# Attention and a gated two-layer network on one core: the places of the tiles in SBUF are taken in another order

## The chip, the core and the metric

The kernel runs on one core of a Trainium2 chip. The metric is the device time in microseconds (us) of one execution. Three executions of the kernel before were timed; their median is the figure to be compared with.

## The reference

Attention over a narrow band and over block summaries comes first, for 4 batches, 8 heads, 768 positions and 64 elements a head; its output, 3072 rows of 512, goes through two matrix products with a softmax and a normalisation between them.

```python
k_sum = k.reshape(B, H, nb, 32, D).max(axis=3)
v_sum = v.reshape(B, H, nb, 32, D).mean(axis=3)
scores_l = where(|i - j| < 16, q @ k.T / sqrt(D), -1e9)
scores_s = q @ k_sum.T / sqrt(D) + log(32)
a = softmax(concatenate([scores_l, scores_s]))
x = a @ concatenate([v, v_sum])          # [3072, 512] after the heads are joined
h = x @ w_in                             # 512 -> 1024
solu = h * softmax(h)
ln = (solu - mean) / sqrt(var + 1e-6) * g_ln
out = ln @ w_out                         # 1024 -> 512
```

All of it is float32.

## The kernel before, in words

The rows are worked in 24 tiles of 128 (`t` from 0 to 23). For each tile there are six pieces of work on TensorE: the scores `s` (line 578), their transposes `t` (line 633), the weighted sum of the values `x` (line 672), the first product `h` (line 697), the transposes `lt` of the normalised rows (line 633 again) and the second product `o` (line 775).

The two products are where float32 accuracy is bought with three passes. Each operand is split into a high and a low part in the type float32r, and three matmuls are added up in PSUM: high data with low weights, low data with high weights, high with high. A matmul has a part that is loaded into the array first, by LDWEIGHTS, and a part that is streamed through it. Here the **data** (`xh`, `xl` for `h`; `lh`, `ll` for `o`; 128 columns, 512 bytes in each partition) are loaded, and the **weights** (`w0` to `w15`; 512 columns, 2048 bytes) are streamed. One tile takes 24 matmuls for `h` and 24 for `o`, so 576 and 576 in all; the last tile's `o` is cut into two column halves, which makes 48 matmuls of 256 columns out of its 24.

`w0` to `w7` are `w_in`, `w8` to `w15` are `w_out`; each tile holds a high half of 2048 bytes and a low half of 2048 bytes, and stands in the place of the raw words it was split from. The data tiles exist twice and are used in turn: `xh` and `xl` change place with every second tile (a group of 256 positions feeds two tiles), `lh` and `ll` with every tile.

The order of all instructions comes from a planner (`Plan`): work is first recorded as operations with an estimated cost, then `issue` orders them, in 64 trials with noise, by these costs, and writes the best order out. While TensorE would have nothing to do early on, `keep_up` writes bfloat16 matmuls of a tile of zeros (`zero`, line 900) to keep it running.

A tile's place in SBUF is taken when its buffer is touched for the first time (`Buf.ap`, line 60, calls the `make` that `Plan.buf`, line 93, stored). So in the kernel before the places follow one another in the order in which the planner wrote the first use of each buffer out, and small tiles of 4 to 192 bytes lie between the large ones. Places are rounded to 32 bytes.

Of the kernel before, what the change touches and what calls it, by code (L numbers as in the profile page):

```python
# [13 lines left out]
BF16 = mybir.dt.bfloat16  # L14
# [6 lines left out]
P = 128  # L21
# [30 lines left out]
class Buf:  # L52


    def __init__(self, make, prev=()):
        self.make, self.prev, self.tile = make, prev, None
        self.ops, self.writers, self.readers, self.gone = [], {}, {}, False
# [15 lines left out]
class Plan:  # L73
# [14 lines left out]
    TRIES, NOISE = 64, 3.0  # L88

    def __init__(self):  # L90
        self.ops, self.rings, self.banks, self.idle = [], {}, {}, None

    def buf(self, pool, shape, dtype, tag, bufs, name):
        ring = self.rings.setdefault(tag, [])
        slot = f"{tag}_{len(ring) % bufs}"
        b = Buf(lambda: pool.tile(shape, dtype, tag=slot, bufs=1, name=name), ring[-bufs:][:1] if len(ring) >= bufs else ())
        ring.append(b)
        return b

    def place(self, make, bank, tag):  # L100

        b = Buf(make, [self.banks[bank]] if bank in self.banks else ())
        self.banks[bank] = b
        self.rings.setdefault(tag, []).append(b)
        return b
# [149 lines left out]
def attn_then_solu(ctx: ExitStack, tc: tile.TileContext, q, k, v, vr, vb, w_in, w_out, g_ln, out):  # L255
# [3 lines left out]
    nc = tc.nc  # L259
    plan = Plan()  # L260
# [13 lines left out]
    const = ctx.enter_context(tc.tile_pool(name="const", bufs=1))  # L274
# [21 lines left out]

    mask = const.tile([P, 3, KC], F32, name="mask")
    g_sb = const.tile([P, NFC], F32, name="g_sb")
    zero = const.tile([P, 512], BF16, name="zero")

    make_identity(nc, ident)
    nc.gpsimd.memset(mhalf, -0.5)
    nc.vector.memset(zero, 0.0)
    nc.gpsimd.memset(mask[:, :, :WIN], 0.0)
    nc.gpsimd.memset(mask[:, :, WIN:], math.log(BLOCK) / SCALE)
    for p0 in (0, QT):
# [531 lines left out]
    for t in range(NT):  # L838
        n, j = divmod(t, 2)
        b, g = its[n]  # L840
# [59 lines left out]
        nc.tensor.matmul(x[:, :n], zero[:, :P], zero[:, :n], start=True, stop=True)  # L900

    plan.idle = idle
    plan.issue()


# [38 lines left out]
```

## Time and profile before

| | |
|---|---|
| median of the three timed executions | 397.99 us (lowest 396.39, highest 946.64) |
| the profiled execution | 397.45 us, its span from first to last instruction 395.7 us |
| TensorE matmuls busy | 386.6 us, 98% of the span |
| weight loads busy | 298.3 us, 75% |
| VectorE, ScalarE, GpSimd busy | 275.4, 248.7, 97.9 us |
| mean granted TensorE clock | 0.999 of full |

PE is TensorE's matmuls, PEld its LDWEIGHTS, DVE is VectorE, ACT ScalarE, POOL GpSimd, SP the engine that issues most loads. A recorded matmul lasts longer than its share of TensorE's time, since matmuls are pipelined: a matmul of 512 columns is recorded with 380 to 400 ns, but the next one starts 216 to 237 ns after it. The time from one start to the next, called the spacing below, is what adds up to the kernel's time. It is read from a stretch of time that begins and ends at matmul starts, as the length of the stretch over the number of matmuls, or of weight loads, in it.

### The profile page before, as it was taken

The page shows a single profiled execution, that of the slowest core. Times are in us where ns is not written, and L with a number is a line of the kernel's source. Part 1 is how long each engine was busy: PE and PEld are TensorE (multiplying, and loading weights), DVE is VectorE, ACT ScalarE, POOL GpSimd, SP SyncE. Part 2 cuts the span into 40 slices and gives each one's busy share as a digit, 9 for nine tenths or more (in the row PEclk, how much of TensorE's full clock was granted, in tenths as well). Part 3 has the DMA queues.
Part 4 walks back from the last instruction along what each step waited for, and adds up shares of the span by engine and source line. Part 5 has one row for each costly group of instructions (what it writes and reads, how often), then busy time and mean ns, then how long its engine had stood idle before and what let it go on. Part 6 is the DMA issues. An engine that isn't in the chain of part 4 may idle for free.

```text
span 395.7 us, 9677 instructions
## 1 busy us (share of the span) xinstructions
PE 386.6 (98%) x3697; PEld 298.3 (75%) x3703; DVE 275.4 (70%) x884; ACT 248.7 (63%) x746; POOL 97.9 (25%) x245
## 2 busy tenths in 40 slices
PE   8999998999999999999999999999999999999996
PEld 3436766677878888878888888878888887878776
DVE  4999998999789866577767657657657654554330
ACT  3889686999798756658558466468466463533411
POOL 4224010416837221236220121221021021101100
PEclk9999999999999999999999999999999999999999
DMA  7999992136277320463330410430310000000011
GB/s 287 411 410 369 409 329 78 56 113 185 70 248 208 113 103 0 141 175 104 123 112 2 150 66 27 156 73 28 108 48 27 2 28 27 16 12 28 27 55 53
DMA packets 14994, 49.24 MB, mean 124 GB/s; under 512 B 1836, under 2 KB 2092, under 8 KB 13412
## 3 DMA queue, kind: packets, MB, share of 16 engines
q1 hardware_dynamic: 11084, 41.89, 30.8%
q10 hardware_dynamic: 3864, 6.74, 4.7%
q8 instruction: 29, 0.48, 0.5%
q14 instruction: 17, 0.14, 0.1%
HBM read 40.11 MB, written 6.29 MB: 117 GB/s over the span
## 4 chain that ended last, share of the span: by engine, by line
PE 85%; DMA 6%; ACT 3%; DVE 2%; issue 1%; ACTq 1%; SPq 1%; DVEq 0%
PE o L775 35%; PE h L697 30%; PE x L672 6%; PE s L578 5%; PE t L633 3%; PE lt L633 3%; DMA st_v<-in_vr 3%; DMA raw<-in_w_in 2%; DMA vt<-vsum 2%; PE vs_ps L459 1%; PE x L900 1%; ACT he L712 1%; DVE he L720 1%; ACT at L281 1%; PE x L664 1%
## 5 line engine op out<-in xcount | busy, mean ns | idle before, releaser
L775 PE MATMUL o<-w,lh 128*128 128x512 f32 (+1 forms) x400 | 128.0, 390 | 0.1
L697 PE MATMUL h<-w,xh 128*128 128x512 f32 x384 | 127.0, 398 | 0.4 <-DVE he L720 0.4
L605 ACT ACTIVATE e<-e,nm 128x120 f32<-128x120 f32 x192 | 73.1, 385 | 25.0 <-DVE nm L597 25.0
L775 PEld LDWEIGHTS o<-w,lh 128*128 128x128 f32 x400 | 74.1, 188 | 18.5 <-issue 2.4
L697 PEld LDWEIGHTS h<-w,xh 128*128 128x128 f32 x384 | 72.1, 188 | 18.9 <-ACT e L605 0.8
L775 PE MATMUL o<-w,ll 128*128 128x512 f32 (+1 forms) x200 | 76.9, 384 | 0.0
L697 PE MATMUL h<-w,xl 128*128 128x512 f32 x192 | 75.6, 394 | 0.0
L707 DVE TENSOR_REDUCE hm<-h 128x1 f32<-128x512 f32 x48 | 32.6, 686 | 42.7 <-PE h L697 42.7
L281 ACT COPY at<-t 120x512 f32<-120x512 f32 x46 | 24.8, 587 | 46.1 <-PE t L633 45.6
L775 PEld LDWEIGHTS o<-w,ll 128*128 128x128 f32 x200 | 37.6, 188 | 6.6
L697 PEld LDWEIGHTS h<-w,xl 128*128 128x128 f32 x192 | 36.1, 188 | 7.5
L597 DVE CUSTOM_DVE_ANT_0 e<-s,mask 128x120 f32<-128x120 f32 x192 | 40.6, 276 | 1.3 <-PE s L578 1.3
L712 ACT ACTIVATE he<-h,hm 128x512 f32<-128x512 f32 x48 | 32.8, 697 | 9.4 <-DVE hm L709 9.4
L605 ACT ACTIVATION_READ_ACCUMULATOR e<-e,nm 128x1 f32 x192 | 36.5, 190 | 0.0
L760 DVE TENSOR_TENSOR ll<-lt,lh 128x512 fp32r<-128x512 f32 x48 | 31.9, 682 | 6.0 <-ACT lh L281 5.8
L739 POOL TENSOR_SCALAR ss<-ss 128x1 f32<-128x1 f32 x24 | 7.1, 297 | 115.0 <-ACT sq L735 114.9
L720 DVE SCALAR_TENSOR_TENSOR he<-h,hz,he 128x512 f32<-128x512 f32 x48 | 34.1, 746 | 0.4
L672 PE MATMUL x<-at,vt 120*64 120x64 f32 (+1 forms) x768 | 28.3, 225 | 1.5 <-ACT at L281 1.5
L672 PEld LDWEIGHTS x<-at,vt 120*64 120x64 f32 (+1 forms) x768 | 24.6, 138 | 6.3 <-ACT at L281 2.8
L288 DVE TENSOR_TENSOR e<-e,z 128x960 f32<-128x960 f32 x23 | 26.6, 1156 | 0.5
L281 ACT CAST lh<-lt 128x512 fp32r<-128x512 f32 x33 | 18.6, 596 | 12.9 <-PE lt L633 10.0
L735 ACT ACTIVATE sq<-he 128x1024 bf16<-128x1024 f32 x24 | 25.2, 1050 | 0.2
(94 smaller groups left out, 499.6 us busy)
## 6 DMA issues: line engine op xcount, KB each, us to landing
vt<-in_v SPq DMA_DIRECT2D x12, 1024.0 KB, 5.4
kraw<-in_k SPq DMA_DIRECT2D x16, 400.0 KB, 9.1
out<-os ACTq DMA_DIRECT2D x23, 256.0 KB, 2.0
qt<-in_q SPq DMA_DIRECT2D x11, 512.0 KB, 5.5
raw<-in_w_in SPq DMA_DIRECT2D x8, 512.0 KB, 10.7
raw<-in_w_out SPq DMA_DIRECT2D x8, 512.0 KB, 9.5
st_v<-in_vr SPq DMA_DIRECT2D x6, 512.0 KB, 12.5
st_v<-in_vb SPq DMA_DIRECT2D x8, 384.0 KB, 3.3
```

Of the source, the lines that this page charges most:

```text
L281: by = {act: lambda: nc.scalar.copy(out=to(), in_=of()), dve: lambda: nc.vector.tensor_copy(out=to(), in_=of()), pool: lambda: nc.gpsimd.t ...
L288: by = {dve: lambda: nc.vector.tensor_tensor(out=to(), in0=a(), in1=b(), op=kind), pool: lambda: nc.gpsimd.tensor_tensor(out=to(), in0=a() ...
L597: nc.vector.tensor_tensor_reduce(out=e.ap[:, n, :], in0=sc.ap[:, j, (2 * i + up) * KC:(2 * i + up + 1) * KC], in1=mask[:, mi, :], scale=-S ...
L605: nc.scalar.activation(out=e.ap[:, n, :], in_=e.ap[:, n, :], func=AF.Exp, bias=nm.ap[:, n:n + 1], scale=-1.0, accum_out=z.ap[:, n:n + 1])
L672: nc.tensor.matmul(xp()[j * D:(j + 1) * D, i, qs], vs.ap[:k, u, cs], at.ap[:k, u % 2, n[j] + u // 2, :], start=not apart, stop=not apart o ...
L697: nc.tensor.matmul(hp.ap, a.ap[:, c, ts], w.ap[:, i], start=(c == 0 and n == 0), stop=(c == NKC - 1 and n == 2))
L707: op(dve, 0.6, lambda i=i, hp=hp: nc.vector.tensor_reduce(out=nms.ap[:, i:i + 1], in_=hp.ap, op=ALU.max, axis=AX.X, negate=True), r=[hp], ...
L712: op(act, 0.71, lambda i=i, hp=hp: nc.scalar.activation(out=part(i), in_=hp.ap, func=AF.Exp, bias=nm.ap, accum_out=zs.ap[:, i:i + 1]), r=[ ...
L720: op(dve, 0.67, lambda i=i, hp=hp: nc.vector.scalar_tensor_tensor(out=part(i), in0=hp.ap, scalar=zs.ap[:, 0:1], in1=part(i), op0=ALU.mult, ...
L735: op(act, 1.13, lambda: nc.scalar.activation(out=sq.ap, in_=e.ap, func=AF.Square, accum_out=ss.ap), r=[e], w=[sq, ss])
L760: op(dve, 0.6, lambda part=part, r=r: nc.vector.tensor_tensor(out=part(lo), in0=tp.ap[:, r], in1=part(hi).bitcast(F32), op=ALU.subtract), ...
L775: nc.tensor.matmul(o.ap[:, cols], a.ap[:, f, :], w.ap[:, i, cols], start=(f == 0 and n == 0), stop=(f == NFC - 1 and n == 2))
```

## The change

`Plan.buf` now also notes each new buffer in a list with its size in bytes for each partition. Before the plan is issued, `lay_out` touches all of them in one go, sorted by the largest power of two up to 2048 that divides the size, largest first. The tile of zeros grows from 1024 to 1952 bytes, of which the first 1024 are used as before, so that the first buffer starts at byte 20,480, a multiple of 2048.

```diff
+        if len(ring) < bufs:
+            self.slots.append((tag, math.prod(shape[1:]) * (2 if dtype == BF16 else 4), b))
...
+    def lay_out(self):
+        for _, _, b in sorted(self.slots, key=lambda x: -math.gcd(x[1], 2048)):
+            b.ap
...
-    zero = const.tile([P, 512], BF16, name="zero")
+    zero = const.tile([P, 976], BF16, name="zero")
...
-    nc.vector.memset(zero, 0.0)
+    nc.vector.memset(zero[:, :512], 0.0)
...
     plan.idle = idle
+    plan.lay_out()
     plan.issue()
```

On every engine the instructions, their order, their shapes and the semaphores that they wait for are the same in both kernels, row for row; places in PSUM are the same too. Only places in SBUF differ. The places of the tiles that the products read, as the two built programs have them (first byte in each partition; the last columns give what is left over after dividing by 256 and by 2048):

| tile | before | over 256, over 2048 | after | over 256, over 2048 |
|---|---|---|---|---|
| `w0`; the others at multiples of 4096 behind it | 19,552 | 96, 1120 | 20,480 | 0, 0 |
| `xh`, `xl`, first place | 186,016 and 190,112 | 160, 1696 | 133,120 and 137,216 | 0, 0 |
| `xh`, `xl`, second place | 208,928 and 213,024 | 32, 32 | 176,128 and 180,224 | 0, 0 |
| `lh`, first place | 110,752 | 160, 160 | 90,112 | 0, 0 |
| `ll`, first place | 115,040 | 96, 352 | 98,304 | 0, 0 |
| `lh`, second place | 127,328 | 96, 352 | 94,208 | 0, 0 |
| `ll`, second place | 143,456 | 96, 96 | 161,792 | 0, 0 |
| `zero` | 18,528 | 96, 96 | 18,528 | 96, 96 |
| `ident` | 16,512 | 128, 128 | 16,512 | 128, 128 |

The tiles for `vt`, `qt`, `he`, `at`, `vsum`, `sq` and `os` stand at multiples of 2048 after the change as well; `kraw`, `e` and `kw`, whose sizes are 6400 and 3840 bytes, at multiples of 256. Before, every tile started at some multiple of 32; of those over 2000 bytes only five stood at a multiple of 128: one of the five places of `he`, one of `kw`, one of `kraw`, one of `os`, and `sq`.

More of the change, by code (lines that the diff above doesn't have):

```diff
@@ L90, in __init__ @@
     def __init__(self):
-        self.ops, self.rings, self.banks, self.idle = [], {}, {}, None
+        self.ops, self.rings, self.banks, self.idle, self.slots = [], {}, {}, None, []
     def buf(self, pool, shape, dtype, tag, bufs, name):
```

## The prediction

> **What bounds the kernel now.** First the page's busy shares, its clock row and its chain of waits, then the groups of TensorE's instructions from 97.2 us on, and all engines from 127.0 to 330.9 us:
>
> ```profile
> PE 386.6 (98%) x3697; PEld 298.3 (75%) x3703; DVE 275.4 (70%) x884; ACT 248.7 (63%) x746; POOL 97.9 (25%) x245
> PEclk9999999999999999999999999999999999999999
> PE 85%; DMA 6%; ACT 3%; DVE 2%; issue 1%; ACTq 1%; SPq 1%; DVEq 0%
> ```
>
> ```profile
> L775 PE MATMUL o<-w,lh 128*128 128x512 f32 x350 | 115.4, 399 | 0.0
> L697 PE MATMUL h<-w,xh 128*128 128x512 f32 x304 | 98.8, 395 | 0.0
> L775 PE MATMUL o<-w,ll 128*128 128x512 f32 x175 | 68.8, 393 | 0.0
> L697 PE MATMUL h<-w,xl 128*128 128x512 f32 x152 | 59.9, 394 | 0.0
> ...
> L775 PE MATMUL o<-w,lh 128*128 128x256 f32 x32 | 5.9, 283 | 0.0
> L775 PE MATMUL o<-w,ll 128*128 128x256 f32 x16 | 4.5, 283 | 0.0
> ```
>
> ```profile
> 127.00:330.90 203.90, 203.89 (x2018) 166.46 (x2017) 139.32 (x465) 124.71 (x401) 45.97 (x120) 1.00 0.23 77
> ```
>
> In the last row the columns are the length, then PE, PEld, DVE, ACT and POOL busy. TensorE is busy for 203.89 of 203.90 us at the full clock, VectorE for 139.32 and ScalarE for 124.71; the idle time ahead of the products (the last column of the groups) is 0.0. So from 97.2 us to the end the time is the sum of the matmuls' spacings, and no other engine's speed counts. In that stretch stand 304 + 152 = 456 matmuls of `h`, 350 + 175 = 525 of `o`, and 48 of half size.
>
> Now the spacing. Each stretch below begins and ends at a matmul's start, so length over the count of weight loads (in brackets) is the spacing. The first is bfloat16 filler of the zero tile, the next two are `h` with the data in the first and in the second place, then `o` twice with the first place, once with the second, and the end of that last one by itself:
>
> ```profile
> 11.59:13.75 2.16, 0.97 (x10) 1.00 1.04 416
> 215.15:220.05 4.90, 3.95 (x21) 1.00 0.14 54
> 229.58:234.39 4.81, 3.94 (x21) 1.00 0.14 55
> 209.59:214.46 4.87, 3.94 (x21) 1.00 0.00 0
> 238.45:243.34 4.89, 3.94 (x21) 1.00 0.00 0
> 224.12:228.90 4.78, 3.94 (x21) 1.00 0.73 303
> 225.27:228.90 3.63, 3.00 (x16) 1.00 0.85 354
> ```
>
> The filler is spaced 2.16/10 = 216.0 ns. The float32r matmuls have as many columns and the same clock, and take 4.90/21 = 233.3, 229.0, 231.9, 232.9 and 227.6 ns, and 3.63/16 = 226.9 at the end of the last. The two stretches of `h` run the same instructions on the same weights; what differs is the data and their place. The weights start 96 bytes over a multiple of 256. Where the data do too (`lh`, `ll` in the second place), the spacing is the lowest; at 160 over, 64 bytes off the weights, it is 233.3; at 32 over, 229.0; and with `lh` at 160 and `ll` at 96, 231.9 and 232.9. So place costs time here, and without any wait.
>
> There is a second part to it. The last tile's halves have 256 columns:
>
> ```profile
> 387.17 0.28 PE L775 MATMUL o<-w,ll 128*128 128x256 f32 x1
> 387.29 0.40 PE L775 MATMUL o<-w,lh 128*128 128x256 f32 x2
> 387.53 0.28 PE L775 MATMUL o<-w,ll 128*128 128x256 f32 x1
> ```
>
> Three start within 387.53 - 387.17 = 0.36 us, 120 ns each, from the same second place. A column then costs (226.9 - 120)/256 = 0.418 ns, 512 of them 213.8, and a float32r matmul has 13.1 ns on top, whatever its size, where the filler has 216.0 - 213.8 = 2.2. And 13.1 ns is 31 columns, near 32, which are 128 bytes of float32r.
>
> **The change part by part.** Instructions, order and waits stay; each term is a change of the spacing.
>
> The unequal part. After the change weights and data all stand at multiples of 2048, in step with one another as `lh` and `ll` in the second place are with `w` now. I take 226.9 ns for this part alone. Today's mean is (233.3 + 229.0)/2 = 231.2 for `h`, and for `o` ((231.9 + 232.9)/2 + 227.6)/2 = 230.0. That is 456 x 4.3 = 2.0 us and 525 x 3.1 = 1.6 us, together 3.6.
>
> The 13.1 ns. What would cost 32 columns once for each matmul, at 256 columns as at 512? My reading, which the trace doesn't show directly: the streamed weights are fetched in pieces of 128 bytes, 32 columns at a time. A run of 2048 bytes that begins 96 bytes into a piece touches 17 pieces, not 16, and a run of 1024 touches 9, not 8. A float32r stream is as fast as such fetching, so the extra piece shows; the filler starts 96 bytes into a piece too, but its columns have half the bytes, so it has time to spare. At a multiple of 128 the extra piece is gone, and the spacing falls to the filler's 216.0. Bounds: from 216.0, the lowest row of all, to 226.9, where nothing of it goes. I take 216.0, as the bracket's two sizes fit it. Sum for both parts: 456 x (231.2 - 216.0) = 6.9 us, 525 x (230.0 - 216.0) = 7.4 us, and 48 halves x (13.1 - 2.2) = 0.5 us, 14.8 us in all.
>
> [...]
>
> Before 97.2 us there are 147 more such matmuls (the products have 576 and 600, halves counted, less the 1029 above), but TensorE waits there for others, so I take nothing; 147 x 15 ns = 2.2 us is the most.
>
> Loads. The start waits for two of them:
>
> ```profile
> 3.16 6.38 DMA raw<-in_w_in
> ...
> 9.56 10.83 DMA st_v<-in_vr
> ```
>
> ```profile
> GB/s 287 411 410 369 409 329 78 56 113 185 70 248 208 113 103 0 141 175 104 123 112 2 150 66 27 156 73 28 108 48 27 2 28 27 16 12 28 27 55 53
> ```
>
> They write tiles that now stand at multiples of 2048. No row shows loads to such places. The full slices run at 369 to 411 GB/s, 10% apart, and 10% of 17.2 us is 1.7 us, either way; I take 0, since 409 to 411 is reached by misplaced tiles. [...]
>
> The small matmuls (`s`, `t`, `lt`, `x`) also read moved tiles:
>
> ```profile
> 235.01 0.61 PE t L633 x16
> 235.63 0.50 PE lt L633 x16
> 236.12 1.08 PE x L672 x32
> 237.21 0.98 PE s L578 x32
> ```
>
> That is 3.2 us a tile. No row shows them in another step with one another; by the share that the place is worth in `h` (233.3 against 229.0, 1.9%), 19 tiles could move by 1.2 us either way. I take 0.
>
> New waits? A tile's steps shorten by 14.8 us/19 = 0.8 us. The tightest chain I find is scores, maxima, exponentials and their scaling on the way to the transposes. The scaling ends 2.6 us ahead of the transposes at 235.01:
>
> ```profile
> 231.29 1.16 DVE L288 TENSOR_TENSOR e<-e,z 128x960 f32<-128x960 f32 x1
> ```
>
> It ends at 232.45; with 0.8 us less there are still 1.8 us, so nothing is late next. If that cover were gone, each us missing would cost a us for each tile.
>
> The profiled execution took 397.45 us with a span of 395.7; the median of the runs is 0.54 above it. From the median: 397.99 - 14.8 = 383.2, so 383.0.
>
> **The rivals.** *Only the unequal part goes.* The 13.1 ns may belong to float32r, or to loading 128 columns of it, wherever the weights start; for this speaks that it is the same at both sizes, and that no row has weights at another place. Then 3.6 us are won: 394.4. Chance 0.32.
>
> *Place is not the cause,* and the two places of the data differ for a reason that the change leaves: 398. [...] Chance 0.10.
>
> *In step is the worst, not the best.* If weights and data begin in the same piece at once, because every tile now begins at a multiple of 2048, each matmul could pay one more piece: 226.9 + 13.1 = 240.0 ns. That is 456 x 8.8 + 525 x 10.0 + 48 x 13.1 = 9.9 us more, 407.9. It decides from a mean of 238.3 ns on, where 1029 x 7.7 ns reach 2%. Against it: data and weights in step are the fastest row today. Chance 0.10.
>
> **How the numbers follow.** My forecast has 0.48. A measurement of this kernel tells about 2% from no change, that is 390.0 and 406.0 us. Faster: 0.48. Slower: 0.08 of the last rival's 0.10. The rest, 0.44, is within 2%. The range leaves out the last two rivals (0.20): low is 383.2 less the 2.2 us of the early matmuls and 1.7 us of loads, rounded to 379; high is the first rival with 1.7 us of slower loads, 396.
>
> **What would show it.** Right: both places of the data give the same spacing in `h` and `o`, 216 ns; the halves 109; small pieces as now; no idle time before the products. The first rival: equal spacings at 227, halves still 120. The second: unequal spacings as now. The third: above 238. I am wrong in the sum, not the mechanism, if idle time of 0.5 us a tile appears before `t` or `x`, or if the spacing settles between 216 and 227, as with pieces of 64 bytes: half the 13.1 ns.

## The result, and the profile after

The changed kernel takes 392.95 us (median of four executions, 392.43 to 393.82), the kernel before 397.39 us, with a fourth execution beside it. The ratio is 0.990, with an interval of 0.988 to 0.992: 1.0% faster, 4.4 us by the medians. By the 2% of the prediction this is no change that counts. The forecast of 383.0 us was wrong; the time is near the 394.4 us of the first rival, within the range. The profiled execution after is the slowest of the four, 393.82 us with a span of 392.1, so the two profiles differ by 395.7 - 392.1 = 3.6 us of span, and it is these that are split up below.

The page's busy shares and its row of bytes moved, for the kernel after:

```profile
PE 383.5 (98%) x3697; PEld 298.3 (76%) x3703; DVE 275.7 (70%) x884; ACT 248.7 (63%) x746; POOL 99.2 (25%) x245
GB/s 286 417 419 382 353 367 89 57 109 176 84 218 238 89 134 2 125 188 112 106 131 2 138 80 27 144 87 28 107 49 28 3 28 27 13 16 28 28 55 54
```

Matmuls lost 3.1 us of busy time; nothing else moved by more than 1.3. The four full slices of the loads are 417 419 382 353 where they were 411 410 369 409 GB/s: three a little more, one less.

The groups of TensorE's instructions from 97 us on show the same counts, and still no idle time ahead of them:

```profile
L784 PE MATMUL o<-w,lh 128*128 128x512 f32 x350 | 114.6, 397 | 0.0
L706 PE MATMUL h<-w,xh 128*128 128x512 f32 x304 | 97.5, 391 | 0.0
...
L784 PE MATMUL o<-w,lh 128*128 128x256 f32 x32 | 5.9, 283 | 0.0
```

Now the stretch from the first of these `h` matmuls to the last `o` matmul, and inside it two tiles, first of the kernel before and then of the kernel after. The columns are length, then PE, PEld, DVE, ACT and POOL busy:

```profile
97.00:392.33 295.33, 295.27 (x2725) 240.43 (x2724) 186.78 (x603) 169.93 (x519) 70.37 (x181) 1.00 0.24 79
215.08:243.98 28.90, 28.90 (x290) 23.64 (x289) 20.13 (x70) 17.20 (x53) 5.24 (x16) 1.00 0.21 74
```

```profile
96.68:388.75 292.07, 291.97 (x2726) 240.34 (x2724) 187.39 (x603) 169.86 (x519) 70.36 (x181) 1.00 0.24 80
213.53:242.09 28.56, 28.56 (x290) 23.64 (x289) 20.11 (x70) 17.05 (x52) 5.11 (x16) 1.00 0.21 75
```

So 295.33 - 292.07 = 3.26 us of the 3.6 lie in this stretch, and the other 0.3 ahead of it. Two tiles take 28.56 instead of 28.90 us. Adding up the time from each matmul's start to the next one's puts the gain in its place:

| from a matmul's start to the next start | before, us | after, us | difference |
|---|---|---|---|
| `h` to `h` | 101.12 | 99.19 | -1.94 |
| `o` to `o` | 123.14 | 121.91 | -1.24 |
| all others | 71.07 | 70.98 | -0.09 |

The differences are taken before rounding. Nearly all of the gain is in the two products. The next rows are stretches of 21 matmuls of the kernel after, read as in the prediction: `o` with the first place of its data, `h`, `o` with the second place, `h`, and `o` with the first place again (columns: length, weight loads and their count):

```profile
208.13:212.91 4.78, 3.94 (x21) 1.00 0.00 0
213.59:218.35 4.76, 3.94 (x21) 1.00 0.14 55
222.41:227.19 4.78, 3.94 (x21) 1.00 0.81 317
227.87:232.63 4.76, 3.94 (x21) 1.00 0.14 55
236.69:241.47 4.78, 3.94 (x21) 1.00 0.00 0
```

4.76/21 is 226.7 ns in both places of `h`, where it was 233.3 and 229.0. 4.78/21 is 227.6 ns in both places of `o`, where it was 231.9 or 232.9 and 227.6. The two places of each pair are equal now, at the level that the best place of all, the second of `o`, had before (`h` so falls below both of its old values), and not at 216 ns. The last tile's halves, in the timeline of TensorE, start as before:

```profile
383.23 0.28 PE L784 MATMUL o<-w,ll 128*128 128x256 f32 x1
383.35 0.40 PE L784 MATMUL o<-w,lh 128*128 128x256 f32 x2
383.59 0.28 PE L784 MATMUL o<-w,ll 128*128 128x256 f32 x1
```

Three in 383.59 - 383.23 = 0.36 us, 120 ns each. And the chain of waits of the kernel after shows the products one behind the other, with the small pieces at their old 1.08 and 0.98 us:

```profile
222.15 5.66 PE o L784 x24
227.81 5.44 PE h L706 x24
...
234.37 1.08 PE x L681 x32
235.45 0.98 PE s L587 x32
```

### The profile page after: what moved, and what is told of

It reads as the page before. It is cut to its first block, busy times and chain, and to the rows that moved or that the text cites. A ratio compares the mean times of both kernels' runs of the same rounds, so it can differ in the third digit from the quotient of the medians.

```text
span 392.1 us, 9677 instructions
## 1 busy us (share of the span) xinstructions
PE 383.5 (98%) x3697; PEld 298.3 (76%) x3703; DVE 275.7 (70%) x884; ACT 248.7 (63%) x746; POOL 99.2 (25%) x245
## 4 chain that ended last, share of the span: by engine, by line
PE 81%; DMA 7%; DVE 6%; ACT 3%; issue 1%; ACTq 1%; SPq 0%; DVEq 0%
PE o L784 35%; PE h L706 29%; PE x L681 5%; PE s L587 4%; PE lt L642 3%; PE t L642 3%; DMA raw<-in_w_in 3%; DMA g_sb<-in_g_ln 2%; DMA vt<-vsum 1%; DMA qt<-in_q 1%; DVE e L606 1%; DVE cv L388 1%; DVE he L729 1%; ACT at L289 1%; DVE cv L296 1%
## 5 line engine op out<-in xcount | busy, mean ns | idle before, releaser
L706 PE MATMUL h<-w,xh 128*128 128x512 f32 x384 | 125.5, 394 | 0.4 <-DVE he L729 0.4
L706 PE MATMUL h<-w,xl 128*128 128x512 f32 x192 | 74.8, 390 | 0.0
L291 POOL COPY kw<-ksum 128x192 f32<-128x192 f32 x21 | 9.3, 445 | 65.8 <-PE s L587 33.4
```

What stands on the lines that cost most here:

```text
L706: nc.tensor.matmul(hp.ap, a.ap[:, c, ts], w.ap[:, i], start=(c == 0 and n == 0), stop=(c == NKC - 1 and n == 2))
```

## The experiments

Two questions are open. First, what about the place counts: the multiple at which an operand starts, or the distance between the loaded and the streamed operand? Both changed together. Second, why did the 13.1 ns stay that the forecast wanted to win?

**All places 96 bytes further.** From the changed kernel, every large tile moves by 96 bytes, so weights and data start 96 over a multiple of 2048, as the weights did before, but in step with one another.

```diff
-    zero = const.tile([P, 976], BF16, name="zero")
+    zero = const.tile([P, 1024], BF16, name="zero")
```

> The changed kernel with every buffer 96 bytes further, so that weights and data stand 96 bytes over a multiple of 2048, as far off as the weights were before, but still in step with one another. Theory (only the distance between loaded data and streamed weights counts): spacing 227 ns in both products, 393 us, no difference from the changed kernel. Rival (the multiple itself counts): up to the 4.4 us lost again, 397.4, spacings above 229.

Measured: 394.15 us, 0.992 of the kernel before [0.991, 0.994]. The whole stretch of the products, then one of `o` and one of `h`:

```profile
95.83:387.94 292.11, 291.98 (x2726) 240.27 (x2725) 187.54 (x603) 169.88 (x519) 70.12 (x181) 1.00 0.25 80
```

```profile
207.29:212.08 4.79, 3.94 (x21) 1.00 0.00 0
212.76:217.52 4.76, 3.94 (x21) 1.00 0.15 55
```

292.11 us is the changed kernel's 292.07, and the spacings are its 227.6 (here 4.79/21 = 228.1) and 226.7. The multiples of 512 and 2048 bytes that the change makes are worth nothing in the products. The median is 1.2 us above the changed kernel's 392.95, but the profiled execution took 393.07 us, so this trace does not hold that difference.

**Weights alone.** From the kernel before, only the zero tile grows. All tiles behind it move together, the weights to multiples of 2048; every distance stays as it was.

```diff
-    zero = const.tile([P, 512], BF16, name="zero")
+    zero = const.tile([P, 976], BF16, name="zero")
...
-    nc.vector.memset(zero, 0.0)
+    nc.vector.memset(zero[:, :512], 0.0)
```

> The kernel before with only the zero tile grown: its weights now start at a multiple of 2048, everything else 928 bytes further in the old order, so that each distance between data and weights is as before. Theory (distance): spacings as before, 233.3 and 229.0 ns in the first product by place, 227.6 to 232.9 in the second, 397.4 us. Rival (the start of the streamed weights counts): 227 ns everywhere, 393.

Measured: 396.1 us, 0.998 [0.997, 0.999]. The stretch of the products, then `h` in its two places:

```profile
96.90:392.16 295.26, 295.24 (x2725) 240.44 (x2725) 186.88 (x603) 169.92 (x519) 70.46 (x181) 1.00 0.24 79
```

```profile
215.08:219.98 4.90, 3.95 (x21) 1.00 0.14 54
...
229.51:234.32 4.81, 3.94 (x21) 1.00 0.14 55
```

The stretch is the kernel before's to 0.1 us, and `h` is at 233.3 and 229.0 ns again. This is the row that the prediction missed: weights at another place, and the same spacing. Where the 0.2% of the ratio comes from is not settled: the profiled execution took 397.26 us, 1.2 above the median, so its trace can't show it.

**Data 64 bytes off.** From the changed kernel, the weights keep their places and everything behind them moves by a tile of 64 bytes.

```diff
-    def lay_out(self):
+    def lay_out(self, pad):
-        for _, _, b in sorted(self.slots, key=lambda x: -math.gcd(x[1], 2048)):
-            b.ap
+        slots = sorted(self.slots, key=lambda x: -math.gcd(x[1], 2048))
+        for w in (True, False):
+            for tag, _, b in slots:
+                if tag.startswith("w") == w:
+                    b.ap
+            if w:
+                pad()
...
-    plan.lay_out()
+    plan.lay_out(lambda: sb.tile([P, 16], F32, name="pad"))
```

> The changed kernel with 64 bytes left free behind the weights, so that weights stand at multiples of 2048 and all data 64 bytes over one, all at multiples of 64. Theory (distance): each float32r matmul of 512 columns takes the 233.3 ns that the first place of the data had before, 1029 x 6.4 ns = 6.6 us more than the changed kernel, 399.6 us, slower than both. Rival (multiples of 64 are enough, or only the weights' start counts): 393.

Measured: 398.48 us, 1.003 of the kernel before [1.002, 1.005]. The stretch, and `o` and `h`:

```profile
95.75:393.13 297.38, 297.38 (x2725) 240.41 (x2725) 187.94 (x603) 169.99 (x519) 70.23 (x181) 1.00 0.23 78
```

```profile
208.99:213.89 4.90, 3.95 (x21) 1.00 0.00 0
214.59:219.49 4.90, 3.95 (x21) 1.00 0.14 54
...
229.15:234.06 4.91, 3.95 (x21) 1.00 0.14 53
```

4.90 and 4.91 over 21 are 233.3 and 233.8 ns in both products and both places. The stretch is 5.3 us longer than the changed kernel's, with weights still at multiples of 2048. The expected 6.6 us took each matmul from the settled 226.9 to 233.3 ns; adding up the starts gives `h` 6.3 ns more, `o` 5.2, and the 47 spacings between halves of 256 columns 2.1 less (117.8 ns, from 119.9). Together the three runs settle the first question: what counts is the distance between data and weights.

**The distance by itself.** Behind the changed kernel's end come blocks of 24 float32r matmuls, 128 columns loaded and 512 streamed, with the start of the loaded operand, of the streamed one, or of both moved. The following experiments that measure a matmul use such blocks too, with other sizes or types; the kernel's own part stays as it is in them, and their whole time says nothing.

```diff
+    def block(name, m, n, loaded, moved, kind=F32R, count=24):
+        x = ps.tile([P, 512], F32, tag="bank0", bufs=1, name=name)
+        flat = lambda w: w.ap.rearrange("p i n -> p (i n)").bitcast(kind)
+        for i in range(count):
+            a, b = flat(wt[(1, 3)[i % 2]]), flat(wt[(0, 2)[i // 2 % 2]])
+            nc.tensor.matmul(x[:m, :n], a[:, loaded:loaded + m], b[:, moved:moved + n],
+                             start=i == 0, stop=i == count - 1)
```

> The changed kernel with 17 blocks of 24 float32r matmuls of 512 columns behind its end, on the weight tiles, with the loaded part (128 columns) moved by a number of bytes against the streamed part, or both moved together. Theory (distance, repeating every 256 bytes): 226.7 ns at distances 0, 256 and 512 and whenever both are moved together; 233 at 64; 229 at 192 (64 the other way); others between 227 and 237. Rival (each one's own start counts): moving both by 32, 64 or 96 bytes costs as much as moving one. My reading of the 13 ns as an extra piece of 128 bytes, already contradicted by the changed kernel's 227 ns, would need a block at 216.

The rows hold the last 16 spacings of a block, so length over 16 is the spacing. The loaded operand moved by 0, 16, 32, 64, 192 and 256 bytes, and at the end both moved by 4 bytes:

```profile
389.23:392.86 3.63, 3.00 (x16) 1.00 0.09 33
447.98:451.61 3.63, 3.00 (x16) 1.00 0.00 0
395.03:398.77 3.74, 3.01 (x16) 1.00 0.00 0
400.96:404.69 3.73, 2.99 (x16) 1.00 0.00 0
424.66:428.32 3.66, 3.00 (x16) 1.00 0.00 0
436.42:440.05 3.63, 3.00 (x16) 1.00 0.00 0
477.21:481.02 3.81, 3.02 (x16) 1.00 0.00 0
```

With all blocks, read from the matmuls' starts in the trace (mean of the settled part):

| loaded operand moved by, bytes | 0 | 4 | 16 | 32 | 64 | 96 | 128 | 160 | 192 | 224 | 256 | 512 |
|---|---|---|---|---|---|---|---|---|---|---|---|---|
| spacing, ns | 226.7 | 232.5 | 226.7 | 233.5 | 233.4 | 234.6 | 233.6 | 233.4 | 228.9 | 233.3 | 226.7 | 226.7 |

The price is back at its lowest at 256 and at 512. These blocks also give the kernel before its numbers. Its `h` had the data 64 bytes past the weights in one place and 64 before them, which is 192 past, in the other: 233.4 and 228.9 here, 233.3 and 229.0 there. Its `o` had `lh` at 64 and `ll` at 0 in the first place; two matmuls of three load `lh`, and (2 x 233.4 + 226.7)/3 = 231.2, where 231.9 and 232.9 were read, so `o` is met only to 0.7 and 1.7 ns. Both operands moved by 32, 64 or 96 bytes settle at 226.7 as well, after about a dozen matmuls. No block comes near 216 ns.

**Sixteen bytes off.** In the blocks a distance of 16 bytes was at 226.7 ns from the second matmul on, while in step the first six spacings of a block are 233, 236, 228, 233, 231 and 226. If that held in the kernel, it would save the six slow ones of each product. From the changed kernel, the four data tiles start 16 bytes into larger tiles; the changed kernel runs beside it once more.

```diff
+        size = math.prod(shape[1:]) * (2 if dtype == BF16 else 4)
+        make = lambda: pool.tile(shape, dtype, tag=slot, bufs=1, name=name)
+        if tag in ("xh", "xl", "lh", "ll"):
+            size = 4352
+            make = lambda: pool.tile([P, 1088], dtype, tag=slot, bufs=1, name=name)[:, 4:1028].rearrange(
+                "p (a b) -> p a b", a=shape[1])
```

> The changed kernel with xh, xl, lh and ll (and the rows of v that share their buffers) 16 bytes over a multiple of 256, weights at multiples of 2048. In the bench a block at a distance of 16 bytes was at 226.7 ns from its second matmul on, a block at distance 0 only from its seventh, 32 ns later in sum. If that holds here, the slower matmuls after each interruption go, in sum 1.0 us of the changed kernel's profile (528 x 0.9 ns in the first product, 496 x 1.2 ns in the second): ratio to the changed kernel 0.9975, spacing 226.7 throughout. Rival (the start matters by itself at 16 bytes, as where both were moved by 16 and took 229.9): 3 us slower than the changed kernel, ratio to before 0.998.

> The changed kernel once more, beside the next one on the same chip. Ratio to before 0.990; spacing 226.7 ns with some slower matmuls after each interruption.

Measured: the changed kernel again at 392.7 us, 0.988 [0.987, 0.990]; with 16 bytes 397.27 us, 1.001 [1.000, 1.002]. Two stretches of `h` in the kernel with 16 bytes, both with the second place of the data, 16 spacings near 186 us and 21 near 229 us:

```profile
186.35:189.98 3.63, 3.00 (x16) 1.00 0.19 72
228.57:233.47 4.90, 3.97 (x21) 1.00 0.14 54
```

3.63/16 is 226.9 and 4.90/21 is 233.3 ns, for the same instructions with the same places. At this distance most groups stay at 233 and a few run at 227, while in step most reach 226.7 within six or seven matmuls and the others within about a dozen. So distance 0 is the one to have, and I found no version faster than the changed kernel.

**Sizes and types.** Blocks in step, with fewer streamed or loaded columns, and with bfloat16 and plain float32, for the second question.

> The changed kernel with 12 blocks of 24 matmuls behind its end, all operands in step: float32r with 512, 384, 256 and 128 columns streamed and 128 loaded, with 96, 64 and 32 loaded and 512 streamed, with 64 loaded and 256 streamed; bfloat16 with 128 and 64 loaded; plain float32 with 128 and 32 loaded. Question: whose are the 13 ns that the change left? [...] Theory F (float32r streaming): 13 ns at every loaded size, 226.7, 226.7, 226.7 for 96, 64, 32, and 66 ns at 128 streamed. bfloat16 at 216 in both.

The last 16 spacings of float32r with 512, 384 and 256 columns streamed, then of bfloat16 and of plain float32 with 512:

```profile
389.31:392.94 3.63, 3.00 (x16) 1.00 0.10 33
394.73:397.51 2.78, 2.78 (x17) 1.00 0.00 0
398.84:400.75 1.91, 1.91 (x17) 1.00 0.00 0
425.98:429.43 3.45, 1.57 (x16) 1.00 0.00 0
448.67:455.54 6.87, 3.04 (x16) 1.00 0.00 0
```

Over 16 that is 226.9, 173.8 and 119.4 ns; to the trace's ns the settled spacings are 226.67, 173.33 and 120.0, each the columns at (226.67 - 173.33)/128 = 0.4167 ns, so 213.3 for 512, plus 13.3. bfloat16 has 215.8, which is 2.5 over the same 213.3. A plain float32 matmul is recorded as two, 48 in a block of 24, and each has 429.2 = 2 x 213.3 + 2.5, with loads as long as float32r's: 3.04/16 = 190 ns, against 3.00/16 = 188. This speaks against the loaded bytes as the owner of the 13.3 ns, but doesn't rule them out, since such a load has nearly twice the time to pass (429.2 ns from one matmul to the next, against 226.67); what float32r alone has here is a stream of 4 bytes a column at one column in 0.4167 ns. With 128 columns streamed the spacing is 111.5 ns, and with 64 loaded and 256 streamed 113.3, which is 6.7 on top and not 13.3: so it isn't simply a fixed cost of float32r either.

**Loaded columns and distance at 64 of them.**

> The changed kernel with 16 blocks of 24 float32r matmuls behind its end: 256 and 384 columns streamed with 32, 64, 96 and 128 loaded, and 512 streamed with 64 loaded at distances of 0 to 224 bytes. Theory C (each 16 bytes loaded cost the stream one column's time, so a quarter of the loaded columns): beyond 0.417 ns a column 3.3, 6.7, 10.0 and 13.3 ns, so 110.0, 113.3, 116.7, 120.0 ns at 256 and 163.3, 166.7, 170.0, 173.3 at 384; at 512 with 64 loaded some distance gives 220. Theory F (fixed for float32r): 120.0 and 173.3 at each, which the 113.3 ns with 64 loaded already speaks against.

256 columns streamed with 32 and with 128 loaded:

```profile
388.43:390.31 1.88, 1.73 (x16) 1.00 0.20 70
...
397.68:399.60 1.92, 1.92 (x17) 1.00 0.00 0
```

32, 64, 96 and 128 loaded columns give 117.7, 113.3, 116.0 and 120.0 ns, which don't grow steadily with the load, and with 384 streamed all four lie between 173 and 175. That the top is a quarter of the loaded columns' time, the reading tried here, is out. With 64 loaded columns and 512 streamed the eight distances give 228.4 to 232.6 ns; in step it is 229.8, and the lowest is at 192 bytes, so with a smaller load being in step isn't the best.

**What is streamed.** Blocks in step, in which the stream goes over its first 64, 16 or 4 columns again and again until there are 512, or takes every other column of 1024 (also 256 columns, 64 rows and 32 rows).

```diff
+    def repeated(n):
+        return lambda b: b[:, :n].rearrange("p (o n) -> p o n", o=1).broadcast_to([b.shape[0], 512 // n, n])
```

> The changed kernel with eight blocks of 24 float32r matmuls behind its end, 512 columns each, loaded and streamed part in step; its own part is left as it is. What is asked is to what the 13.3 ns of a float32r matmul belong that are left when nothing is out of step (spacing 226.7 ns against 213.3 ns for the columns alone). all_cols streams 512 columns one behind the other, as before: 226.7 ns. rep_a, rep_b, rep_c and rep_d stream the first 256, 64, 16 and 4 columns again and again until there are 512; step_two streams every other column of 1024. Theory S (the 13.3 ns are spent on the bytes that are fetched for the stream): the fewer columns are repeated, the nearer to 216 ns, at the latest in rep_c and rep_d, and step_two, which touches twice as many bytes, takes more than 226.7 ns. Theory M (they belong to the float32r matmul and its load, whatever it streams): 226 to 228 ns in all six. rows_a and rows_b load and stream 64 and 32 of the 128 rows: by S, if all rows' bytes count together, less than 226.7 ns; by M, 226.7 ns.

64, 16 and 4 columns repeated, then every other column:

```profile
400.37:404.00 3.63, 3.00 (x16) 1.00 0.00 0
406.24:410.12 3.88, 3.04 (x16) 1.00 0.00 0
412.20:415.68 3.48, 3.03 (x16) 1.00 0.00 0
419.36:426.62 7.26, 3.32 (x16) 1.00 0.00 0
```

226.9, 242.5, 217.5 and 453.8 ns. With 4 columns, 16 bytes, the matmul has 217.1 ns (from the starts), 3.8 over its columns: nearly all of the 13.3 is gone, so it isn't part of every float32r matmul (theory M), but hangs on what the stream fetches (theory S). But S wanted 16 columns to be cheap too, and they are the dearest, 242.2; and with every other column the spacing doubles, from 226.7 to 453.3, top included. 64 rows settle at 226.7 like 128; so do 32 rows until the granted clock fell to half in the block's last matmuls (0.50 from 437.8 to 439.4 us). What is streamed moves the spacing, from 217.1 to 453.3 ns with the same load; no more than that is shown.

**Fewer columns by small steps.** The settled spacings up to then in step with 128 loaded and 256, 384 or 512 streamed were multiples of 13.33 ns (the 111.5 ns at 128 streamed, which the expectation passes over, is not), so the 13.3 could be a rounding up, of which 504 columns would pay less.

> The changed kernel with twelve blocks of 24 float32r matmuls behind its end, 128 columns loaded, both parts in step; its own part is left as it is. The columns streamed are 512, 510, 508, 504, 500, 496, 488, 484, 480, 448, 250 and 240 (cols_all, cols_a to cols_k). In the runs so far every settled spacing in step with 128 loaded columns was the columns at 0.4167 ns each plus 13.3 ns: 226.67 at 512, 173.33 at 384, 120.0 at 256, all of them multiples of 13.33 ns (32 columns' time). Theory M (a matmul costs a fixed 13.3 ns): the spacing falls by 0.4167 ns a column: 225.8 at 510, 225.0 at 508, 223.3 at 504, 221.7 at 500, 220.0 at 496, 216.7 at 488, 215.0 at 484, 213.3 at 480, 200.0 at 448, 117.5 at 250, 113.3 at 240. Theory Q (a matmul costs the 2.5 ns that bf16 shows, and the next one starts on the next multiple of 13.33 ns): 226.67 from 512 down to 507, and 213.33 at once from 504 down to 480 (504, 500, 496, 488, 484 and, with 2.5 ns on 200.0, 480 too); 200.0 at 448 by neither; 200.0 at 448 by M and 200.0 by Q (186.7 + 2.5, next multiple); 106.67 + 13.33 = 120.0 at 256 and 106.67 at 250 by Q only, where M has 117.5; 240 gives 113.3 by M and 106.67 by Q. The price of one matmul in the kernel would be rounded up by 10.8 ns by Q, and not be a cost of the matmul.

512, 500, 480 and 240 columns streamed:

```profile
389.12:392.74 3.62, 3.00 (x16) 1.00 0.09 33
412.25:415.88 3.63, 3.02 (x16) 1.00 0.00 0
434.94:438.40 3.46, 3.00 (x16) 1.00 0.00 0
448.13:449.92 1.79, 1.79 (x17) 1.00 0.00 0
```

From the starts: 226.7 at 512, 226.9 at 510, 228.0 at 508, 226.7 at 504 and at 500, 223.5 at 496, 225.7 at 488, 218.7 at 484, 216.4 at 480, 206.7 at 448, 116.8 at 250 and 112.0 at 240. The rounding (213.3 from 504 down) is out: no count reaches 213.3. A fixed 13.3 (221.7 at 500, 213.3 at 480, 200.0 at 448) is wrong too, by 3 to 7 ns: counts below 512 pay 12 to 22 ns on top. 512 columns are no worse a choice than their neighbours.

## Why the prediction was right and wrong

*The bound* was read rightly: TensorE does not idle in the products (busy for 295.27 of 295.33 us before, for 291.97 of 292.07 after), and the time is the sum of their spacings before and after.

*The unequal part* was right in mechanism and nearly in size. It was to give 2.0 us in `h` and 1.6 in `o`; it gave 1.94 and 1.24. The 0.4 missing in `o` comes from the value of 226.9 ns for all 525 matmuls: that is the settled end of a group, but each group begins with slower ones, and its mean was 227.6 already where data and weights were in step. 525 x (230.0 - 227.6) is 1.3 us. That `h` came out so near is partly luck: its mean spacing was 232.5 ns before and 228.0 after, each 1.1 to 1.3 above the values of the sum, and the two errors cancel.

*The 13.1 ns* is the step that failed: 11.2 of the 14.8 us, and nothing of it came. The step was a reading that no row showed: a run of 2048 bytes that begins inside a piece of 128 bytes touches one piece more. With everything at multiples of 2048 the top is still 226.7 - 213.3 = 13.3 ns, with everything 96 bytes over it is the same, and with the weights alone at multiples of 2048 every spacing is as before. The quoted rows could not carry the step: the two sizes showed that the top is there once for each matmul, which fits the first rival as well, and the filler at 216.0 differs from the products in its type, not in its place. The lowest row of all was a price for bfloat16. What the top belongs to is open: it goes down to 3.8 ns when the stream stays within 16 bytes, and no simple rule of bytes, of loaded columns or of rounding gives the other numbers.

*Loads and small pieces* at nothing: right within what the profile tells. The full slices moved by -14 to +4% with no common sign, and everything beside `h` and `o` by 0.09 us of 71.

*New waits:* none, right; with 0.2 us won for a tile instead of 0.8 the cover was not even touched.

*The rivals.* The first, that only the unequal part goes, is what happened: equal spacings at 227, halves at 120, 394.4 forecast and 392.95 measured. Its chance of 0.32 was below that of a step without a row of its own. The second falls with the 64 bytes: distance alone moves the products by 5.3 us. In the blocks, 233.4 against 226.7 ns by 64 bytes of distance alone says the same of loaded and streamed operand. The third, in step as the worst, falls with every row in step.

One thing isn't settled: by medians the change is worth 4.4 and, repeated, 397.17 - 392.7 = 4.5 us, by the two profiles 3.6, of which the products are 3.2. The products repeat: their stretch is 292.07 us in the profile of the changed kernel run again (97.01 to 389.08 us), too. What varies is where it starts, 95.6 to 97.0 us in the seven profiles of kernels without blocks, 96.7 and 97.0 in the two of the changed kernel. The remaining 1 us or so may lie there; no trace of an execution near the median shows it.

## What to carry to other kernels

Where float32r matmuls of 512 streamed columns follow one another with a new load of 128 columns each, place the loaded and the streamed operand at the same byte within 256 (226.7 ns in the blocks, against 228.9 to 234.6 at distances of 32 to 224 bytes); it costs an order of allocation and 928 bytes here, and was worth 1 to 3% of such a matmul, while the absolute multiple (0 or 96 bytes over 2048) was worth nothing in the products (292.07 and 292.11 us). It is no rule for other sizes: with 64 columns loaded (228.4 ns at 192 bytes, 229.8 in step), and with 256 streamed (117.8 at 64 bytes, 119.9 in step), some other distance was faster by 1 to 2 ns. When a forecast takes a lower spacing from another instruction as its goal, ask in what else that instruction differs: the filler's 216.0 ns was a price for bfloat16, and no float32r product of 512 columns settled below 226.7 here. And if one condition was never varied in the trace (here the weights' place), the term that needs it deserves a lower chance than the rival that needs nothing.

## What was not expected of the hardware

- Distance between loaded and streamed operand counts, and its price was back at the lowest after 256 bytes: 226.7 ns at 0, 256 and 512, 233.3 to 234.6 at 32 to 160 and at 224, 228.9 at 192, in blocks of 128 columns loaded and 512 streamed, with everything else equal.
- In the kernel with a distance of 16 bytes the same instructions ran at 226.9 ns in one group and at 233.3 in another, where the block at 16 bytes had 226.7.
- Both operands moved by 4 bytes: 237.8 ns; both by 16 bytes: 229.9; both by 32, 64 or 96: 226.7 once settled. So at 4 and 16 bytes the absolute start does count.
- float32r has 13.3 ns on top of its columns at 512, 384 and 256 where bfloat16 and plain float32 have 2.5 at 512; float32r has 3.8 when the stream repeats 16 bytes, but 28.9 when it repeats 64 bytes.
